# Unit 0's window mask as a bias added by matmuls, zero matmuls that wait for results, and a new order of work

## The chip, the cores and the metric

The kernel runs on one core of one Trainium2 chip. The metric is the device time of one execution in microseconds (us). Before the change three runs gave 165.78, 166.09 and 166.78 us, so the median is 166.09 us.

The engines are named as the profile names them: PE (TensorE matmul), PEld (its weight load), DVE (VectorE), ACT (ScalarE), POOL (GpSimd) and SP (SyncE, which here only starts transfers).

## The reference

Attention with 4 sink keys and a window of 128 keys, for 4 batches, 8 heads, 768 positions and heads of 64, and then a channel mix on the attention's output:

```python
scores = q @ k.T / 8
keep = (key < 4) | ((0 <= query - key) & (query - key < 128))
a = softmax(where(keep, scores, -1e9));  x = a @ v          # x: [4, 768, 512]
x_prev = x shifted by one position, zeros first
xk = mu_k * x + (1 - mu_k) * x_prev;  xr = mu_r * x + (1 - mu_r) * x_prev
k = relu(xk @ w_k);  v = (k * k) @ w_v;  out = sigmoid(xr @ w_r) * v
```

`w_k` is 512 x 1024, `w_v` is 1024 x 512, `w_r` is 512 x 512. All inputs and the output are float32; the kernel multiplies in bfloat16.

## The kernel before

**Units.** The work is cut into 12 units of 256 positions, three for each batch (T = 0, 1, 2). For each unit u the kernel does four steps.

- `prepare(u)`: k and q arrive in float32 (tiles ks, qs), are cast to bfloat16 (kb, qb), and are transposed into kt and qt. For early units PE transposes and an engine copies the result out of PSUM (lines 726 and 721); from unit 5 (k) and 7 (q) on a DMA transposes. v is cast to vb (line 740).
- `attend(u)`: for each of four pairs of heads, scores into a PSUM tile `sc` (line 815), exp on ACT (line 887, tile e), a product with a 0/1 mask on DVE (line 901), probabilities times values on PE (line 920), a reciprocal and a scaling on DVE (lines 934 and 937, tile x). A unit with T = 0 has a mask of 384 columns for each of two heads (`mask0`), the others one of 256 columns repeated. Sink keys go their own small way (lines 784, 791, 858 or 873).
- `mix(u)`: x is transposed (line 961, copied out at line 970 into xt), then differences td (line 997) and the fused multiply-adds xk and xr (line 1010), all on DVE.
- `ffn(u)`: keys (line 1087), relu (line 1097 on ACT or 1101 on DVE), square (line 1109, DVE), gate (line 1118), tanh (line 1124, ACT), product with w_v (line 1136), and the gating (line 1145, DVE), then the store (line 1152). The second half of the last unit is cut in two column parts (`last_product`, lines 1046 to 1074): 128 columns first, then 384.

The weights come as float32 and are cast by pieces: four of w_k and two of w_r (lines 620 and 626), four of w_v (lines 620 and 624).

**Order.** Nothing is issued where the code defines it. Every step is registered with `P.op` under a running number. `CHOICE` (line 18) gives an engine to the numbers that may run on several, and `ORDER` (line 72) has, for each of PE, DVE, ACT, POOL and SP, the complete sequence of numbers by hand. `Plan.schedule` (line 187) merges these five sequences with estimated costs, hands out the buffers on the way, and each engine then runs its own sequence strictly in order, waiting for semaphores where a step needs another engine's result.

**Zero matmuls.** Where the plan sees PE idle for more than 300 ns (600 ns early on) before 26 us of its own clock, it puts in matmuls of a zero tile `warm` (lines 1160 to 1166) into a free PSUM bank. They wait for no result; they only keep PE running.

**Constants.** POOL builds the identity, the masks, and small tiles for the sinks at the start, in the order mask0, identity, hmask, mask, spread, and casts the second half of unit 0's k after them. DVE clears tiles in `fill` and `fill_later` (lines 525 to 537, some 2 us).

The code of `BIAS` (line 38, the function `biased`, the functions `make_bias0` and `first_mask`) is there before the change, but the tuple is empty, so no unit uses it.

Of the kernel before, what the change touches and what calls it, by code (L numbers as in the profile page):

```python
# [18 lines left out]
    80: "ACT", 81: "POOL", 82: "ACT", 83: "POOL", 84: "POOL", 85: "ACT", 86: "ACT",  # L19
    88: "ACT", 90: "DVE", 96: "POOL", 98: "DVE", 99: "DVE", 101: "DVE", 102: "ACT",  # L20
    103: "ACT", 129: "POOL", 132: "DVE", 135: "POOL", 141: "ACT", 144: "DVE", 151:
    "DVE", 160: "PE/full", 172: "PE/full", 183: "POOL", 186: "DVE", 189: "POOL",
    192: "POOL", 195: "ACT", 196: "DVE", 198: "DVE", 242: "PE/full", 265: "DVE",
    268: "DVE", 271: "POOL", 273: "DVE", 274: "POOL", 277: "DVE", 278: "ACT", 352:
    "POOL", 355: "POOL", 361: "DVE", 380: "DVE", 428: "POOL", 432: "POOL", 438:
    "ACT", 496: "PE/full", 511: "POOL", 516: "ACT", 517: "ACT", 587: "POOL", 591:
    "ACT", 592: "ACT", 628: "POOL", 661: "POOL", 663: "POOL", 665: "ACT", 666:
    "ACT", 675: "DVE", 736: "POOL", 741: "ACT", 785: "POOL", 810: "POOL", 815:
    "DVE", 855: "POOL", 888: "DVE", 889: "ACT", 929: "POOL", 945: "PE/full", 998:
    "DVE", 1002: "DVE", 1006: "DVE", 1010: "DVE", 1019: "POOL",  # L30
# [7 lines left out]
BIAS = ()  # L38
# [56 lines left out]
    ),  # L95
    "DVE": (
# [25 lines left out]
    ),  # L122
    "ACT": (
# [14 lines left out]
    ),  # L138
    "POOL": (
# [3 lines left out]
    ),  # L143
# [8 lines left out]
    ),  # L152
}


class Plan:

    SEM = 40.0
    LAG = {"PE": 163.0, "DVE": 83.0, "ACT": 114.0, "POOL": 60.0, "SP": 90.0}

    def __init__(self):
        self.ops, self.pools, self.buf = [], {}, {}
        self.fill, self.fill_until = None, 0.0  # L170

# [15 lines left out]
    def schedule(self):  # L187
# [43 lines left out]
        while any(lines.values()):  # L231
# [35 lines left out]
            if o["port"]:  # L267
                port[o["engine"]] = t + (0.58 * cost if o["engine"] == "POOL" else cost)
# [953 lines left out]
```

## Time and profile before

| what | value |
|---|---|
| median of three runs | 166.09 us |
| the profiled execution | 166.53 us |
| its span, first to last instruction | 164.4 us |
| PE busy | 152.6 us, 93% of the span |
| DVE busy | 149.5 us, 91% |
| ACT busy | 121.7 us, 74% |
| POOL busy | 31.7 us, 19% |
| matmuls, weight loads | 1819, 1838 |

The profiled execution has 2.13 us around its span and is 0.44 us above the median. Numbers of the trace are compared within that one execution.

The page gives the busy time of each engine, the span in 40 slices with the busy tenths of each engine and the clock that was granted to PE, the DMA queues, the chain of waits that ended last, and the costliest groups of instructions. A matmul's recorded time is a latency: 512 columns take 379 ns from start to end, but eight of them follow one another in 1.73 us. So a PE that looks busy still has some room.

### The profile page before, as it was taken

The numbers are of one execution on the slowest core, as the hardware profiler recorded it, in microseconds if no ns is written. First come the engines' busy times: TensorE is split into PE (matmuls) and PEld (weight loads), VectorE is DVE, ScalarE is ACT, GpSimd is POOL, SyncE is SP. The second block draws the span as 40 slices with busy tenths as digits, with TensorE's granted clock in tenths as the row PEclk, the third lists the DMA queues.
The fourth block names the chain that finished last, engine by engine and source line by source line (L and its number), as shares of the span: only waits on it lengthen the run. The fifth ranks groups of instructions, "written<-read, shape, count | busy, mean of one in ns | idle before, by whom it ended". The sixth has DMA issues, their size and how long they took to land.

```text
span 164.4 us, 4647 instructions
## 1 busy us (share of the span) xinstructions
PE 152.6 (93%) x1819; PEld 101.1 (61%) x1838; DVE 149.5 (91%) x383; ACT 121.7 (74%) x198; POOL 31.7 (19%) x61
## 2 busy tenths in 40 slices
PE   7988678899989999999999999999999999999991
PEld 2445557675448658677666766855485756578450
DVE  2599999999999999999999999998899989999931
ACT  3789989999989999999997689782499695152020
POOL 6633341312422023220201001032000100101001
PEclk9999789999999999999999999999999999999999
DMA  5999998999899999889988998999999933251032
GB/s 145 249 357 278 394 333 215 366 394 322 193 271 272 260 219 221 160 176 162 270 216 207 233 232 215 220 219 128 235 165 191 268 94 96 54 205 64 0 144 112
DMA packets 78821, 35.16 MB, mean 214 GB/s; under 512 B 68744, under 2 KB 71056, under 8 KB 78800
## 3 DMA queue, kind: packets, MB, share of 16 engines
q1 hardware_dynamic: 78384, 33.56, 84.0%
q0 software_dynamic: 400, 1.31, 2.3%
q8 instruction: 14, 0.23, 0.6%
q14 instruction: 7, 0.06, 0.1%
q10 hardware_dynamic: 16, 0.00, 0.0%
HBM read 24.12 MB, written 6.29 MB: 185 GB/s over the span
## 4 chain that ended last, share of the span: by engine, by line
PE 62%; DVE 24%; DMA 4%; POOL 4%; issue 3%; ACT 1%; DVEq 0%; POOLq 0%
PE bank L1087 21%; PE bank L1136 18%; PE bank L1118 8%; PE bank L920 6%; DVE e L901 5%; DMA kt<-kb 4%; PE sc L815 4%; DVE xr L1010 3%; DVE xk L1010 3%; DVE x L937 3%; DVE kk L1109 2%; DVE td L997 2%; PE bank L873 1%; POOL hmask L543 1%; PE bank L1057 1%
## 5 line engine op out<-in xcount | busy, mean ns | idle before, releaser
L1087 PE MATMUL bank<-xk,wk_sb 128*128 128x256 bf16 x384 | 47.6, 273 | 1.1 <-ACT rl L1097 0.5
L887 ACT ACTIVATE e<-sc 128x1024 bf16<-128x1024 f32 (+1 forms) x48 | 44.5, 967 | 2.8 <-PE sc L815 2.5
L1136 PE MATMUL bank<-wv_h,kk 128*128 128x512 bf16 x171 | 43.8, 379 | 0.8 <-DVE xk L1010 0.2
L1087 PEld LDWEIGHTS <-wk_sb 128*128 128x128 bf16 x384 | 36.2, 98 | 7.7 <-issue 1.5
L1097 ACT ACTIVATE rl<-bank 128x512 bf16<-128x512 f32 x43 | 25.2, 607 | 8.3 <-PE bank L1087 7.8
L901 DVE TENSOR_TENSOR e<-e,mask 128x1024 bf16<-128x1024 bf16 (+1 forms) x48 | 30.8, 656 | 0.0
L1124 ACT ACTIVATE th<-bank 128x512 f32<-128x512 f32 x24 | 14.3, 612 | 18.2 <-PE bank L1118 11.4
L1136 PEld LDWEIGHTS <-kk 128*128 128x128 bf16 x184 | 17.0, 98 | 16.5 <-issue 0.2
L1010 DVE SCALAR_TENSOR_TENSOR xr<-td,mu_all,xt 128x256 bf16<-128x256 bf16 x48 | 23.8, 507 | 0.0
L1118 PE MATMUL bank<-wr_sb,xr 128*128 128x512 bf16 x90 | 23.3, 379 | 0.3
L1010 DVE SCALAR_TENSOR_TENSOR xk<-td,mu_all,xt 128x256 bf16<-128x256 bf16 x48 | 23.3, 511 | 0.0
L1109 DVE TENSOR_TENSOR kk<-rl 128x512 bf16<-128x512 bf16 x48 | 19.8, 425 | 0.4 <-ACT rl L1097 0.2
L937 DVE TENSOR_TENSOR x<-bank,rec 128x256 bf16<-128x256 f32 x48 | 19.5, 418 | 0.4
L920 PE MATMUL bank<-vb,e 128*128 128x65 bf16 x352 | 16.8, 196 | 1.4 <-DVE e L901 1.1
L1145 DVE SCALAR_TENSOR_TENSOR ob<-th,bank 128x512 f32<-128x512 f32 x23 | 15.6, 681 | 1.9 <-PE bank L1136 1.1
L920 PEld LDWEIGHTS <-e 128*128 128x128 bf16 x352 | 14.2, 99 | 4.5 <-DVE e L901 1.9
L1118 PEld LDWEIGHTS <-xr 128*128 128x128 bf16 x96 | 9.0, 98 | 9.6
L815 PE MATMUL sc<-qt,kt 64*64 64x128 bf16 (+3 forms) x496 | 12.5, 226 | 0.1
L1152 POOL DMA_DIRECT2D out_dram<-ob x5 | 2.8, 570 | 46.8 <-DVE ob L1145 46.8
L815 PEld LDWEIGHTS <-kt 64*64 64x64 bf16 (+1 forms) x496 | 9.0, 106 | 3.3 <-issue 1.0
L997 DVE TENSOR_TENSOR td<-xt 128x512 bf16<-128x512 bf16 x24 | 10.1, 432 | 0.1
L663 POOL CAST kb<-ks 128x512 bf16<-128x512 f32 x6 | 5.3, 884 | 20.4 <-DMA ks<-in_k_dram 17.8
(87 smaller groups left out, 157.2 us busy)
## 6 DMA issues: line engine op xcount, KB each, us to landing
vs<-in_v_dram SPq DMA_DIRECT2D x24, 256.0 KB, 5.3
out_dram<-ob SPq DMA_DIRECT2D x18, 256.0 KB, 3.3
ks<-in_k_dram SPq DMA_DIRECT2D x16, 256.0 KB, 4.2
qs<-in_q_dram SPq DMA_DIRECT2D x12, 256.0 KB, 4.9
qs<-in_q_dram SPq DMA_DIRECT2D x6, 512.0 KB, 7.1
ks<-in_k_dram SPq DMA_DIRECT2D x4, 512.0 KB, 9.3
w<-in_moe_w_k_dram SPq DMA_DIRECT2D x2, 1024.0 KB, 8.6
w<-in_moe_w_v_dram SPq DMA_DIRECT2D x2, 1024.0 KB, 10.6
```

The costliest lines, as they stand in the source:

```text
L815: nc.tensor.matmul(out=sc[keys, a, o0 + f0 - q0:o0 + f1 - q0], lhsT=lhs[rows, keys], rhs=qs[rows, f0:f1], start=u not in BIAS, stop=True, ...
L887: nc.scalar.activation(out=buf[ek][:, :, lo:], in_=buf[sck][:, :, lo:], func=AF.Exp, scale=scale)
L901: nc.vector.tensor_tensor(out=at, in0=at, in1=m, op=ALU.mult)
L920: nc.tensor.matmul(out=o[:, g, a, :], lhsT=e[:, a, e0:e0 + 128], rhs=rhs, start=(T == 0 and i == 0), stop=(i == len(blocks) - 1), skip_gro ...
L937: P.op("DVE", dve(256), lambda ok=ok, rk=rk, c=c: nc.vector.tensor_tensor(out=buf["x", u][:, :, 128 * c:128 * c + 128].rearrange("p g (a d ...
L1010: nc.vector.scalar_tensor_tensor(out=buf[key][:, c, :], in0=buf[tk][:, i, :], scalar=mu[w][:, c:c + 1], in1=xt[:, c, t0 - 1:t0 + 255], op0 ...
L1087: nc.tensor.matmul(out=ps[:, i, :], lhsT=wk_sb[:, c, 128 * f:128 * f + 128], rhs=xk[:, c, :], start=(c == 0), stop=(c == NC - 1), skip_gro ...
L1097: nc.scalar.activation(out=buf[rk], in_=buf[psk].rearrange("p (i t) -> p i t", i=2), func=AF.Relu)
L1109: P.op("DVE", dve(512, 0.52), lambda f2=f2, rk=rk: nc.vector.tensor_tensor(out=buf["kk", u][:, 2 * f2:2 * f2 + 2, :], in0=buf[rk], in1=buf ...
L1118: nc.tensor.matmul(out=buf[psk], lhsT=buf["xr", u][:, c, 128 * g:128 * g + 128], rhs=wr_sb[:, c, :], start=(c == 0), stop=(c == NC - 1))
L1136: nc.tensor.matmul(out=buf[psk], rhs=wv_h[:, f, :], lhsT=buf["kk", u][:, f, 128 * g:128 * g + 128], start=(f == 0), stop=(f == NF - 1))
L1145: P.op("DVE", dve(512), lambda psk=psk, tk=tk, bk=bk: nc.vector.scalar_tensor_tensor(out=buf[bk], in0=buf[tk], scalar=1.0, in1=buf[psk], o ...
```

## The change

- `BIAS = (0,)`: for unit 0 POOL builds a tile `bias0` of 384 columns (0 where a key is seen, -30000 where not) in a buffer of `ob` that is used much later. For each pair of score tiles PE first multiplies the identity with that tile into `sc`, two matmuls for each score tile, eight in all, and the score matmuls add to it. The four mask products of unit 0 on DVE are gone. `mask0` is still made, for units 3, 6 and 9, after unit 0's cast on POOL, and so are `mask` and `spread`.
- Zero matmuls from 4.6 us of the plan's clock on can have a `gate`: the moving operand is then not the zero tile but a tile that a step on DVE or ACT has just written, so that the matmul waits for that step. The stationary operand stays zero. They may go into a free bank or a free score tile. The plan leaves 130 ns behind each (`PAUSE`), and goes on with them to 28.5 us of its clock.
- Costs of the plan: POOL casts 600 instead of 620 ns, weight casts on POOL 1050 instead of 1100, a store from POOL 600 instead of 1100, DMA transposes 2250 (k) and 1450 (q) instead of 1950.
- `CHOICE` and all five sequences of `ORDER` are new. SP's first 15 transfers keep their order; from there on the loads of w_r and w_v stand behind more loads of k, q and v.

The numbers after 72 are shifted by one, those after unit 0's attention by minus one. With that taken out, these steps change their engine (counts over the whole kernel, before and after):

| step (line) | ACT | DVE | POOL |
|---|---|---|---|
| mask product (901) | | 48, 44 | |
| cast of unit 0's k, q (668) | 1, 3 | 2, 0 | 1, 1 |
| cast of k, q, units 1 to 4 and q of 5, 6 (659) | 7, 8 | 4, 2 | 9, 10 |
| cast of k, q of DMA-transposed units (663) | 16, 15 | 0, 1 | 8, 8 |
| copy of kt, qt (721) | 19, 18 | 1, 2 | |
| cast of v (740) | 14, 13 | 4, 2 | 6, 9 |
| cast of w_k, w_r (626) | 3, 2 | | 3, 4 |
| cast of w_v (624) | 2, 3 | 2, 1 | |
| copy of xt (970) | 9, 10 | 5, 4 | |
| relu (1096) | 43, 42 | 5, 6 | |

The first-half copies of unit 0's kt and qt (line 726) go from ACT to DVE and the second-half ones from DVE to ACT. Seven stores instead of five start from POOL. In the last unit the 384-column part now stands ahead of the 128-column part.

```diff
-BIAS = ()
+BIAS = (0,)
...
+    PAUSE = 130.0
...
+        done = {}
...
+                own.append((b[0], name, b[1], None))
...
-            if o["engine"] == "PE" and self.fill:
+            if o["engine"] == "PE" and self.fill and before < 4600.0:
...
+            elif o["engine"] == "PE" and self.fill and before < self.fill_until:
+                last = max((j for j in o["after"]), key=lambda j: ops[j]["end"], default=None)
+                now, seen = before, before - 500.0
+                while now + 230.0 < t:
+                    some = [(b[0], name, b[1], b) for name in ("bank", "sc") for b in free[name]
+                            if b[0] <= now] + [b for b in own if b[1] in ("bank", "sc") and b[0] <= now]
...
+                    gates = [j for j, e in done.items() if seen < e + self.SEM <= now and (
+                        last is not None and ops[j]["engine"] == ops[last]["engine"] or
+                        e < t - 700.0)]
+                    gate = max(gates, key=lambda j: done[j], default=None)
...
+                    order.append(("fill", tile_ if name == "bank" else tile_[:, 0, :], 1, gate))
+                    now += 225.0
...
+                    now += self.PAUSE if gate is not None else 0.0
+            if o["engine"] in ("DVE", "ACT") and self.gate(i):
+                done[i] = end
...
+    def part(i):
...
+        if name == "wk":
+            return lambda: wk_sb[:, 0, 256 * u:256 * u + 128]
...
+        if name == "xt":
+            t0 = 16 + 256 * key[2]
+            return lambda: xts[u][:, 2 * key[3], t0:t0 + 128]
...
+    def fill(bank, wide, gate=None):
+        if gate is not None:
+            nc.tensor.matmul(out=bank, lhsT=warm[:, 0:128], start=True, stop=True,
+                             rhs=part(gate)().unsqueeze(1).to_broadcast([128, 4, 128]))
...
-    P.fill_until = 26000.0
+    P.fill_until = 28500.0
```

More of the change, by code (lines that the diff above doesn't have):

```diff
@@ L18 @@
 CHOICE = {
[L19 to L30, printed above, removed]
+    81: "ACT", 82: "POOL", 83: "POOL", 84: "POOL", 85: "ACT", 86: "POOL", 87: "ACT",
+    89: "ACT", 90: "ACT", 93: "DVE", 96: "DVE", 97: "POOL", 104: "ACT", 128: "DVE",
+    134: "POOL", 137: "POOL", 141: "ACT", 171: "PE/full", 182: "POOL", 185: "POOL",
+    187: "DVE", 194: "ACT", 195: "DVE", 197: "DVE", 204: "DVE", 216: "DVE", 253:
+    "PE/full", 264: "POOL", 267: "POOL", 270: "DVE", 275: "DVE", 276: "ACT", 282:
+    "DVE", 289: "DVE", 345: "POOL", 348: "POOL", 354: "POOL", 358: "ACT", 396:
+    "POOL", 404: "PE/full", 427: "POOL", 428: "POOL", 431: "DVE", 436: "ACT", 437:
+    "ACT", 510: "POOL", 515: "ACT", 584: "POOL", 585: "POOL", 590: "ACT", 627:
+    "POOL", 631: "POOL", 703: "POOL", 734: "POOL", 735: "POOL", 740: "ACT", 741:
+    "ACT", 771: "DVE", 780: "POOL", 813: "ACT", 814: "DVE", 841: "DVE", 858:
+    "PE/full", 881: "POOL", 885: "POOL", 888: "ACT", 924: "POOL", 944: "PE/full",
+    977: "DVE", 994: "POOL", 1001: "DVE", 1005: "DVE",
 }
@@ L254, in schedule @@
             lines[o["engine"]].pop(0)
+            own = []
             for name, key in o["take"]:
@@ L267, in schedule @@
             if o["port"]:
-                port[o["engine"]] = t + (0.58 * cost if o["engine"] == "POOL" else cost)
+                port[o["engine"]] = t + (max(0.58 * cost, cost - 200.0) if o["engine"] == "POOL" else cost)
             end = t + cost + o["lag"]
@@ L311, in schedule @@
                     order.append(("fill", self.pools["bank"][b[1]], wide))
+            elif o["engine"] == "PE" and self.fill and before < self.fill_until:
[4 more added lines that the diff above has]
+                            if b[0] <= now] + [b for b in own if b[1] in ("bank", "sc") and b[0] <= now]
+                    if not some:
+                        now += 60.0
+                        continue
+                    _, name, at_, b = min(some, key=lambda b: b[:3])
+                    tile_ = self.pools[name][at_]
+                    gates = [j for j, e in done.items() if seen < e + self.SEM <= now and (
[3 more added lines that the diff above has]
+                    if gate is not None:
+                        seen = done[gate] + self.SEM
+                    order.append(("fill", tile_ if name == "bank" else tile_[:, 0, :], 1, gate))
+                    now += 225.0
+                    if b is not None:
+                        free[name].remove(b)
+                        free[name].append((now, at_))
+                    now += self.PAUSE if gate is not None else 0.0
+            if o["engine"] in ("DVE", "ACT") and self.gate(i):
+                done[i] = end
             order.append(i)
@@ L630, in cast @@
                    "ACT": (act(1024), emit("ACT"), False)} |
-             ({} if half else {"POOL": (1100.0, emit("POOL"), True)}),
+             ({} if half else {"POOL": (1050.0, emit("POOL"), True)}),
              reads=[(name + "32", i)], writes=writes)
@@ L676, in prepare @@
                            "DVE": (341.0, cast(nc.vector.tensor_copy), True),
-                           "POOL": (620.0, cast(nc.gpsimd.tensor_copy), True)},
+                           "POOL": (600.0, cast(nc.gpsimd.tensor_copy), True)},
                      take=[] if half else [(name + "b", rk)],
@@ L1155, in ffn @@
                  alts={"SP": (400.0, store(nc.sync), False),
-                       "POOL": (1100.0, store(nc.gpsimd), True)})
+                       "POOL": (600.0, store(nc.gpsimd), False)})
     zeros = warm.bitcast(FP32)
-    def fill(bank, wide):
-        if wide == 1:
+    def part(i):
+        o = P.ops[i]
+        key = o["writes"][0] if o["writes"] else ()
+        if not isinstance(key, tuple) or len(key) < 2:
+            return None
+        name, u = key[0], key[1]
+        if name == "wk":
+            return lambda: wk_sb[:, 0, 256 * u:256 * u + 128]
+        if name == "wr":
+            return lambda: wr_sb[:, 2 * u, 0:128]
+        if name == "wv":
+            return lambda: wv_h[:, 2 * u, 0:128]
+        if name == "e" and o["engine"] == "DVE":
+            return lambda: buf[key][:, 0, 384:512]
+        if name in ("kb", "qb") and not by_dma(name[0], u):
+            if octet(name[0], u):
+                return lambda: eights(buf[key[:2]])[:, 4 * key[2]].rearrange("p h d -> p (h d)")
+            return lambda: buf[key[:2]][:, 0, 4 * key[2]:4 * key[2] + 2, :].rearrange(
+                "p h d -> p (h d)")
+        if name == "x":
+            return lambda: buf["x", u][:, 0, 128 * key[2]:128 * key[2] + 128]
+        if name == "xt":
+            t0 = 16 + 256 * key[2]
+            return lambda: xts[u][:, 2 * key[3], t0:t0 + 128]
+        if name == "td":
+            return lambda: buf[key][:, 0, 0:128]
+        if name in ("xk", "xr") and len(key) == 3:
+            return lambda: buf[key[:2]][:, key[2], 0:128]
+        if name == "rl":
+            return lambda: buf[key][:, 0, 0:128]
+        if name == "kk":
+            return lambda: buf["kk", u][:, 2 * key[2], 0:128]
+        return None
+    def fill(bank, wide, gate=None):
+        if gate is not None:
+            nc.tensor.matmul(out=bank, lhsT=warm[:, 0:128], start=True, stop=True,
+                             rhs=part(gate)().unsqueeze(1).to_broadcast([128, 4, 128]))
+        elif wide == 1:
             nc.tensor.matmul(out=bank, lhsT=warm[:, 0:128], start=True, stop=True,
```

11 lines of the change are left out of this document (6 added, 5 removed), and 140 rows, old and new, of the table ORDER.

## The prediction

> **What bounds the kernel now.** I read the page's head and its 40 slices first, then the busy time of each engine by stage, because shares over the whole span mix stages.
>
> ```profile
> span 164.4 us, 4647 instructions
> PE 152.6 (93%) x1819; PEld 101.1 (61%) x1838; DVE 149.5 (91%) x383; ACT 121.7 (74%) x198; POOL 31.7 (19%) x61
> PEclk9999789999999999999999999999999999999999
> ...
> 0.00:9.55 9.55, 8.04 (x37) 3.64 (x37) 4.76 (x21) 5.72 (x9) 5.83 (x24) 1.00 0.83 209
> 9.55:45.36 35.81, 30.59 (x425) 21.52 (x427) 35.40 (x85) 32.93 (x53) 11.98 (x17) 0.95 1.04 318
> 45.36:100.00 54.64, 53.53 (x734) 37.24 (x742) 53.99 (x141) 49.48 (x84) 8.60 (x11) 1.00 1.02 221
> 100.00:157.00 57.00, 56.54 (x606) 36.77 (x612) 53.85 (x138) 32.76 (x55) 4.77 (x9) 1.00 0.70 155
> ```
>
> The columns of the stages are length, then busy PE, PEld, DVE, ACT, POOL, granted clock, DMA share, GB/s. I cut where the chain of waits changes hands: from DVE's first mask product (9.55 us) to its first `ob` (45.36) nearly all its links are DVE. There DVE is busy 35.40 of 35.81 us and ACT 32.93, so ACT has 2.9 us to spare; PE idles 5.2 us. From 45.36 to 100 PE idles 1.1 and DVE 0.65 us: both are full. After 100 only PE is. So a microsecond saved on DVE counts up to 45 us, is shared with PE to 100, and hardly counts later; POOL is nearly free throughout.
>
> What feeds the start is data:
>
> ```profile
> 3.87 0.51 DVE L668 CAST kb<-ks 128x512 bf16<-128x512 f32 x1 [2.04 <-DMA ks<-in_k_dram]
> 4.59 1.04 DVE L531 MEMSET vsink<- 128x520 bf16 x2
> 6.27 0.43 DVE L668 CAST qb<-qs 128x512 bf16<-128x512 f32 x1
> 7.24 0.61 POOL L668 CAST kb<-ks 128x512 bf16<-128x512 f32 x1 [1.29 <-DMA ks<-in_k_dram]
> 8.34 0.69 DVE L726 COPY kt<-bank 128x512 bf16<-128x512 bf16 x1 [1.64 <-PE bank L708]
> 8.95 0.68 DVE L726 COPY qt<-bank 128x512 bf16<-128x512 bf16 x1
> 9.55 0.55 DVE L901 TENSOR_TENSOR e<-e,mask 128x768 bf16<-128x768 bf16 x1
> 10.82 1.16 POOL L659 CAST kb<-ks 128x512 bf16<-128x512 f32 x2 [1.21 <-DMA ks<-in_k_dram]
> 21.06 1.04 POOL L626 CAST wk_sb<-w 128x1024 bf16<-128x1024 f32 x1 [2.23 <-DMA w<-in_moe_w_k_dram]
> 24.34 0.38 PE L1087 MATMUL bank<-xk,wk_sb 128*128 128x256 bf16 x2
> ```
>
> The casts wait for k's halves at 3.87 and 7.24 us, for unit 1's k at 10.82 and for w_k at 21.06, and the first FFN matmul stands at 24.34. SP's first 15 transfers are unchanged, so these dates stay.
>
> **DVE's sum.** The moved steps have one price each by form:
>
> ```profile
> L901 DVE TENSOR_TENSOR e<-e,mask 128x768 bf16<-128x768 bf16 x16 | 8.9, 572 | 0.0
> L740 DVE CAST vb<-vs 128x512 bf16<-128x512 f32 x4 | 1.7, 420 | 0.0
> L970 DVE COPY xt<-bank 128x512 bf16<-128x512 bf16 x5 | 2.0, 410 | 0.0
> L721 DVE COPY kt<-bank 128x512 bf16<-128x512 bf16 x1 | 0.7, 677 | 0.0
> L624 DVE TENSOR_SCALAR wv_h<-w 128x1024 bf16<-128x1024 f32 x2 | 1.4, 682 | 0.0
> L1101 DVE TENSOR_SCALAR rl<-bank 128x512 bf16<-128x512 f32 x5 | 3.3, 686 | 0.3 <-PE bank L1087 0.3
> L740 ACT CAST vb<-vs 128x512 bf16<-128x512 f32 x14 | 8.7, 635 | 0.5 <-DMA vs<-in_v_dram 0.4
> ```
>
> (I give the L740 price, 0.42, to the equal casts of L659 and L663.) Following both sequences up to the first `ob`, DVE loses four masks (2.29), unit 0's two casts (0.51 + 0.43), five casts of q of units 1 to 3, k of 3 and v of 3 (2.10), three copies of xt (1.23), one of kt (0.68), a piece of w_v (0.68) and a relu (0.69): 8.61 us. It gains two casts of k (0.84; units 1 and 3), two copies of qt (1.36), three of xt (1.23), a relu (0.69) and one cast of unit 5 (0.42): 4.54. The copies of unit 0's kt and qt are exchanged one for one. Net -4.1 us.
>
> Of this, what DVE did before 10.8 us saves nothing. In the new sequence it waits from `fill` for kt's transposes (about 5 us), copies kt and qt, only then clears its tiles (2 us, over by 8.5), and the next step is the cast of unit 1's k, which lands at 10.8. In that time the old order had done the two casts and two masks of unit 0 (0.94 + 1.1); so 2.0 of the 4.1 us are lost in a wait, and **-2.1 us** is left.
>
> **POOL's price on DVE.** The new order puts casts on POOL. What that does is seen here:
>
> ```profile
> L1010 DVE SCALAR_TENSOR_TENSOR xr<-td,mu_all,xt x48: 456/477/1250, 16.5 to 152.9; 128x256 bf16<-128x256 bf16 x48
> ...
> 21.13 1.25 DVE L1010 SCALAR_TENSOR_TENSOR xr<-td,mu_all,xt 128x256 bf16<-128x256 bf16 x1
> ...
> 17.20 1.63 POOL L659 CAST kb<-ks 128x512 bf16<-128x512 f32 x2 [0.89 <-DMA ks<-in_k_dram]
> ...
> 17.23 1.12 DVE L901 TENSOR_TENSOR e<-e,mask 128x1024 bf16<-128x1024 bf16 x1
> 18.28 0.41 DVE L970 COPY xt<-bank 128x512 bf16<-128x512 bf16 x1
> ```
>
> Beside the cast of w_k (1.04 us from 21.06) a DVE step with a median of 0.477 takes 1.25, so 0.77 is lost; the mask beside a small cast takes 1.12 against 0.68 elsewhere, 0.44 lost; the copy out of PSUM at 18.28 keeps its 0.41 beside the same POOL work. Up to 45 us POOL has 16 casts in place of 14, one of the two extra ones a weight: 0.77 + 0.44 = **+1.2 us**. `mask0` and `mask` also move to after 11 us (1.7 us of POOL work by the rows at L543 and L562 below); DVE's steps there read PSUM (L934, L937), which lose nothing, so I take 0, with +1.0 as the other end.
>
> [...] Taken at full length for each POOL microsecond, the two casts and the moved masks would be 1.6 + 1.7 = 3.3 us and not 1.2; that case is the third rival.
>
> **ACT.** Up to 45 us ACT gets 16 small steps and gives up 13, at 0.6 us (the L740 row) +1.8, and two weight pieces change against two others. Its spare 2.9 us falls to about 1.0. So even if DVE gained more, ACT lets little over 1 us through. Most of what it takes on belongs to units 0 to 2, ahead of 24 us, where its rows (below, at 16 to 24) already show 3.83 and 3.29 busy of 4.
>
> **PE.** The eight bias matmuls:
>
> ```profile
> 1.29 0.80 POOL L543 TENSOR_SCALAR_AFFINE_SELECT mask<-ones 128x128 bf16<-128x128 bf16 x3 [0.77 <-DVE ones L527]
> 2.05 0.30 POOL L562 MEMSET mask<- 4x256 bf16 x1
> 9.35 0.38 PE L1162 MATMUL bank<-warm 128*128 128x512 bf16 x1
> 159.41 1.46 PE L1057 MATMUL bank<-wv_h,kk 128*128 128x384 bf16 x8
> 160.91 0.55 DVE L1067 SCALAR_TENSOR_TENSOR ob<-th,bank 128x384 f32<-128x384 f32 x1 [0.55 <-PE bank L1057]
> ```
>
> Eight of 384 columns take 1.46 us (the row at 159.41, same width), half ahead of each pair of scores, in time that zero matmuls fill today (9.35). They need only the identity and `bias0` (0.80 + 0.30 on POOL, in `mask0`'s old place): 0, and 0.7 if the second four stand behind a late POOL. PE's first step is now the small transpose of mu; its two 2 KB loads are issued at 1.1 and 1.7 us, and everything PE does waits behind it: 0, up to +0.5.
>
> Zero matmuls with a wait: behind each stands all of PE's queue, so the next real step can lose the 0.38 us of L1162 or, if the awaited result is late, the lateness. PE's idle 5.2 us in the stage from 9.55, at 0.36 us a piece (225 + 130 ns in the plan), hold about 14 of them. Between nothing (all in real gaps) and 14 x 0.38 = +5.3 (all on the path) I take 0, nearest to DVE's row: it is full to 45 us and hides what PE does late by less than its queue. They could also gain:
>
> ```profile
> 16.00:20.00 4.00, 2.39 (x52) 2.12 (x52) 4.00 (x8) 3.83 (x7) 1.94 (x3) 0.83 1.05 396
> 20.00:24.00 4.00, 2.93 (x55) 2.18 (x53) 3.85 (x11) 3.29 (x6) 1.27 (x2) 0.74 1.10 360
> ```
>
> Clock 0.83 and 0.74 lose (0.17 + 0.26) x 4 = 1.7 us of PE's time, but DVE is idle 0.15 us in those 8, so at most 0.15 comes back: 0. [...] If PE were the path there, the sum would be 1.7 us lower.
>
> **Later steps.** Loads of w_r and w_v stand behind 2 to 6 more loads on SP. The first product with w_v moves from PE's place 70 to 92, so the later data has cover; without it a PE wait of some us. Stores move between SP and POOL late, where both are idle: 0. After 45 us DVE's net change is nil and ACT's -1.9: 0, with 1.5 either way for an order that differs everywhere. At the end 128 columns stand last in place of 384: the last DVE step shrinks from 0.55 us to about 0.29 (same step, other part): **-0.2**.
>
> **The sum.** -2.1 + 1.2 - 0.2 = -1.1 us, and the -0.9 of it that lies on DVE is just what ACT's spare 1.0 lets through. The profiled execution (166.53) becomes 165.4; it lies 0.44 above the median, so I forecast **165.0**, with a range of its own from 164.2 to 165.9.
>
> **Rivals.**
> - *More goes through (faster).* DVE's 2.0 us before 10.8 return because unit 0's x is ready without masks, and the steadier clock gives PE its 1.7 us at 16 to 24. For it: DVE's total falls 4 us and both engines are full to 100 us. Against: ACT. -4.1 + 1.2 - 0.2 = -3.1 is 163.0 against the median; with 0.7 of the clock's share it is 162.3, with only half of the 2.0 returned 164.0. So 162.3 to 164.2. Chance 0.30.
> - *The waiting zero matmuls hold PE (slower).* Where real results run later than the plan by more than a gap, all 14 block scores and values, ACT's exps start later, and ACT has no slack to catch up. Half of them at 0.38 is 2.7 us, all 5.3; less the 1.1: 167.7 to 170.3. It decides (slower by over 1%) once more than 7 of them cost their full length. For it: ACT full to 24 us, strict order. Against: DVE's queue. Chance 0.24.
> - *POOL holds DVE, nothing is gained.* With 3.3 for 1.2 the sum is +1.0: 166.0 to 167.2. The 0.41 us copy at 18.28 speaks against it. Chance 0.10.
>
> **The numbers.** Forecast 0.36, of which 0.05 lies under 164.4. About 1% (1.7 us) is what a measurement here tells from no change. Faster: 0.30 + 0.05; slower: 0.23 of the second rival's 0.24; the rest is the same. The range leaves out a tenth at each end: 162.4 to 168.2.
>
> **What would show it.** In the new profile: four fewer mask steps; DVE idle about 2 us before 10.8; stage 16 to 24 at clock 1.00; the first FFN matmul still at 24 to 25; DVE steps at L1010 over 1 us beside weight casts; PE idle under 1.1 us in the 55 us after the first `ob`. I am wrong if PE waits on ACT or DVE in rows of the zero matmuls, if ACT's waits for scores grow, or if PE's idle time after 45 us moves by over 1.5 us.

## The result, and the profile after

The changed kernel takes **171.86 us** (median of six runs), the kernel before 165.94 us on the same chip: ratio 1.0319, 95% interval 1.0272 to 1.0366. It is slower by 3.2%, about 5.3 us. The ratio is taken without the executions in which the chip was in a slower state, 1 to 2% longer here, so it is not the quotient of the two medians. The forecast was 165.0 us with a range up to 168.2, so both the sign and the range were wrong. The profiled execution has a span of 170.2 us against 164.4. In the new file the lines are those of before plus 30 (the mask product is line 931, the exp 917, the scores 845); the biased products are line 854, the zero matmuls with a wait line 1226, those without 1229 and 1232.

The head of the page and its clock row:

```profile
span 170.2 us, 4708 instructions
PE 156.0 (92%) x1845; PEld 102.2 (60%) x1865; DVE 149.3 (88%) x374; ACT 121.3 (71%) x198; POOL 38.4 (23%) x72
...
PEclk9999999999999999999999999999999999999999
```

The clock is now full throughout, and DVE's busy time over the whole kernel is what it was (149.5). The same stages as before, with the same columns (length, busy PE, PEld, DVE, ACT, POOL, granted clock, DMA share, GB/s):

```profile
0.00:9.55 9.55, 6.12 (x29) 3.12 (x29) 4.08 (x19) 3.40 (x6) 5.00 (x19) 1.00 0.80 192
9.55:45.36 35.81, 31.08 (x454) 21.50 (x453) 31.50 (x73) 32.88 (x54) 16.66 (x30) 1.00 1.09 327
45.36:100.00 54.64, 52.91 (x708) 35.06 (x717) 52.55 (x132) 49.53 (x82) 9.54 (x14) 1.00 0.93 200
100.00:157.00 57.00, 56.06 (x601) 37.03 (x608) 54.61 (x139) 33.83 (x56) 6.16 (x10) 1.00 0.79 164
```

Between 9.55 and 45.36 us DVE is busy 31.50 us where it was busy 35.40. The four microseconds that were to be saved are there, but as idle time, and the kernel is late. The first stage shows why to look at the start: ACT is busy 3.40 us instead of 5.72, among others because the first exps have all but left it. The timeline of that start (start, duration, engine, line, operation; in brackets the idle time before it and what ended it):

```profile
5.77 0.69 DVE L756 COPY kt<-bank 128x512 bf16<-128x512 bf16 x1 [3.93 <-PE bank L738]
6.45 0.69 DVE L756 COPY qt<-bank 128x512 bf16<-128x512 bf16 x1
...
7.35 1.04 DVE L561 MEMSET vsink<- 128x520 bf16 x2
...
8.75 0.31 DVE L567 MEMSET sc<- 64x128 f32 x2
...
9.11 0.51 PE L845 MATMUL sc<-qt,kt 64*128 64x256 bf16 x8 [1.83 <-DVE sc L567]
...
9.48 1.51 ACT L917 ACTIVATE e<-sc 128x768 bf16<-128x768 f32 x2 [2.09 <-PE sc L845]
...
11.29 0.43 DVE L689 CAST kb<-ks 128x512 bf16<-128x512 f32 x1 [2.17 <-DMA ks<-in_k_dram]
```

kt and qt of the first scores are there at 7.14 us. But the scores are written to a tile of which DVE clears a corner, and this clear (0.31 us, line 567) stands last in `fill_later`, which the new order places behind the two copies. So the first scores start at 9.11 us. By the code, unit 0's scores and exps use only the columns from 128 on, and the clear those from 64 to 127: the scores wait for the tile, not for values that they need. Before, the same rows were:

```profile
6.00 0.31 DVE L537 MEMSET sc<- 64x128 f32 x2
6.48 0.51 PE L815 MATMUL sc<-qt,kt 64*128 64x256 bf16 x8
6.86 1.51 ACT L887 ACTIVATE e<-sc 128x768 bf16<-128x768 f32 x2 [0.43 <-PE sc L815]
```

The first exp is 2.6 us late. In the list of PE's waits (columns: engine, line waited for, total, times, longest) this one stands first, and those of the waiting zero matmuls are small:

```profile
PE sc L845 <- DVE sc L567: 1.8, 1, 1.8
PE bank L950 <- DVE vb L770: 1.7, 2, 1.2
...
PE bank L1226 <- DVE xr L1040: 0.6, 1, 0.6
```

The 2.6 us don't explain 5.3 by themselves. Following DVE's written order through the traces gives the dates at which its last scaling of a unit (the `x` step) ends:

| kernel | unit 0 | unit 1 | unit 2 | unit 5 | unit 9 | last `ob` of all |
|---|---|---|---|---|---|---|
| before | 17.3 | 26.9 | 38.8 | 74.9 | 116.5 | 161.5 |
| after | 15.9 | 27.5 | 42.4 | 81.5 | 123.5 | 167.2 |
| a_sc_early (below) | 13.8 | 24.6 | 37.8 | 76.7 | 119.7 | 162.1 |
| b_fill_early (below) | 17.5 | 26.2 | 38.4 | 74.8 | 116.1 | 162.0 |
| b_sc_late (below) | 22.1 | 30.7 | 42.9 | 79.2 | 120.4 | 165.3 |
| b_pool21 (below) | 17.4 | 26.2 | 38.2 | 78.2 | 121.2 | 166.8 |
| b_bias (below) | 17.1 | 26.9 | 39.7 | 75.7 | 117.2 | 162.1 |

(Old and new order take the units in different turns, so rows of one order are to be compared with each other.)

### The profile page after: what moved, and what is told of

The parts are those of the page before. It is cut to its first block, busy times and chain, and to the rows that moved or that the text cites. A ratio compares the mean times of both kernels' runs of the same rounds, so it can differ in the third digit from the quotient of the medians.

```text
span 170.2 us, 4708 instructions
## 1 busy us (share of the span) xinstructions
PE 156.0 (92%) x1845; PEld 102.2 (60%) x1865; DVE 149.3 (88%) x374; ACT 121.3 (71%) x198; POOL 38.4 (23%) x72
## 4 chain that ended last, share of the span: by engine, by line
PE 61%; DVE 25%; ACT 6%; issue 3%; DMA 2%; DVEq 0%; ACTq 0%
PE bank L1166 21%; PE bank L1117 17%; PE bank L1148 9%; DVE e L931 7%; PE bank L950 5%; PE sc L845 4%; DVE xk L1040 3%; DVE xr L1040 3%; DVE x L967 3%; ACT e L917 3%; DVE kk L1139 2%; DMA ob<-in_moe_mu_k_dram 2%; PE bank L991 1%; DVE td L1027 1%; DVE rec L964 1%
## 5 line engine op out<-in xcount | busy, mean ns | idle before, releaser
L917 ACT ACTIVATE e<-sc 128x1024 bf16<-128x1024 f32 (+1 forms) x48 | 45.0, 963 | 6.7 <-PE sc L845 5.0
L1117 PE MATMUL bank<-xk,wk_sb 128*128 128x256 bf16 x384 | 48.8, 273 | 0.6 <-DVE xk L1040 0.3
L931 DVE TENSOR_TENSOR e<-e,mask 128x1024 bf16<-128x1024 bf16 (+1 forms) x44 | 31.3, 715 | 0.8 <-ACT e L917 0.8
L1127 ACT ACTIVATE rl<-bank 128x512 bf16<-128x512 f32 x42 | 24.3, 606 | 9.9 <-PE bank L1117 9.0
L1040 DVE SCALAR_TENSOR_TENSOR xk<-td,mu_all,xt 128x256 bf16<-128x256 bf16 x48 | 24.8, 534 | 0.1
L1040 DVE SCALAR_TENSOR_TENSOR xr<-td,mu_all,xt 128x256 bf16<-128x256 bf16 x48 | 24.4, 518 | 0.0
L950 PE MATMUL bank<-vb,e 128*128 128x65 bf16 x352 | 17.2, 193 | 2.4 <-DVE vb L770 1.7
L950 PEld LDWEIGHTS <-e 128*128 128x128 bf16 x352 | 14.5, 97 | 6.0 <-issue 2.2
L845 PE MATMUL sc<-qt,kt 64*64 64x128 bf16 (+4 forms) x496 | 12.6, 226 | 2.3 <-DVE sc L567 1.8
L1182 POOL DMA_DIRECT2D out_dram<-ob x7 | 3.9, 564 | 44.1 <-DVE ob L1175 38.0
L770 POOL CAST vb<-vs 128x512 bf16<-128x512 f32 x9 | 6.5, 728 | 24.2 <-DMA vs<-in_v_dram 24.1
L964 DVE RECIPROCAL rec<-bank 128x4 f32<-128x4 f32 x48 | 7.9, 172 | 3.3 <-PE bank L950 2.6
```

The costliest lines, as they stand in the source:

```text
L845: nc.tensor.matmul(out=sc[keys, a, o0 + f0 - q0:o0 + f1 - q0], lhsT=lhs[rows, keys], rhs=qs[rows, f0:f1], start=u not in BIAS, stop=True, ...
L917: nc.scalar.activation(out=buf[ek][:, :, lo:], in_=buf[sck][:, :, lo:], func=AF.Exp, scale=scale)
L931: nc.vector.tensor_tensor(out=at, in0=at, in1=m, op=ALU.mult)
L950: nc.tensor.matmul(out=o[:, g, a, :], lhsT=e[:, a, e0:e0 + 128], rhs=rhs, start=(T == 0 and i == 0), stop=(i == len(blocks) - 1), skip_gro ...
L1040: nc.vector.scalar_tensor_tensor(out=buf[key][:, c, :], in0=buf[tk][:, i, :], scalar=mu[w][:, c:c + 1], in1=xt[:, c, t0 - 1:t0 + 255], op0 ...
L1117: nc.tensor.matmul(out=ps[:, i, :], lhsT=wk_sb[:, c, 128 * f:128 * f + 128], rhs=xk[:, c, :], start=(c == 0), stop=(c == NC - 1), skip_gro ...
```

## The experiments

Names that begin with a_ are made from the changed kernel, those with b_ from the kernel before. Where an old order is used with the new code, its numbers are mapped to the new numbering.

### Is it the place of the clear, or is it the zero matmuls, the bias, the order?

a_sc_early is the changed kernel with nothing altered but the place of the two clears:

```diff
     def fill():
         for t, value in ((ones, 1.0), (spread, 0.0), (hmask, 1.0)):
             nc.vector.memset(t, value)
+        for t in P.pools["sc"]:
+            nc.vector.memset(t[0:64, :, 64:128], 0.0)
 
     def fill_later():
...
-        for t in P.pools["sc"]:
-            nc.vector.memset(t[0:64, :, 64:128], 0.0)
```

> The changed kernel, with the two clears of the score tiles (0.31 us on DVE) moved from the end of fill_later to the end of fill, ahead of the copies of kt and qt. Late start theory: the first scores no longer wait for DVE (1.8 us in the changed kernel), the first exp starts at about 7.2 us and not 9.5, and the whole is 1.0 to 2.5 us shorter. If POOL's casts or the zero matmuls are the cause, the first exp comes early but the whole changes by under 0.7 us.

Measured: 167.38 us, ratio 1.0075 (1.0038 to 1.0112). Moving a clear of 0.31 us takes back 2.4 of the 3.2%. Its timeline:

```profile
1.86 0.31 DVE L559 MEMSET sc<- 64x128 f32 x2
...
6.95 0.51 PE L845 MATMUL sc<-qt,kt 64*128 64x256 bf16 x8
...
7.32 1.51 ACT L917 ACTIVATE e<-sc 128x768 bf16<-128x768 f32 x2 [0.49 <-PE sc L845]
```

The scores come 2.2 us earlier than in the changed kernel, unit 0's `x` 2.1, unit 1's 2.9, unit 2's 4.6 us; from there to the end the distance stays between 3.8 and 5.1. So the lateness of the start more than doubles between 25 and 42 us.

a_no_zero leaves the changed kernel as it is, without a zero matmul after 4.6 us:

```diff
-    P.fill_until = 28500.0
+    P.fill_until = 0.0
```

> The changed kernel without any zero matmul after 4.6 us of the plan's clock. If the zero matmuls that wait hold PE, the whole is 2 to 5 us shorter. If they lie in real gaps, it is the same within 0.7 us or, since PE's clock can then fall in the first 30 us, up to 1.5 us longer.

Measured: 171.70 us, ratio 1.0315 (1.0229 to 1.0401), the same as with them. The clock of PE falls (to 0.51 from 20 to 24 us), and in the whole this costs nothing that these runs can tell. Unit 1's `x` ends at 28.2 us instead of 27.5, as DVE waits longer for PE (the row `DVE rec L964 <- PE bank L950` has 3.7 us between 11 and 43 us, against 2.0 in the changed kernel), but unit 2's ends at 42.4 in both:

```profile
20.00:24.00 4.00, 2.91 (x43) 2.47 (x43) 3.45 (x8) 3.80 (x6) 1.11 (x1) 0.51 1.05 390
```

b_bias is the kernel before with the bias alone, b_zero the changed code in the old order without the bias (so that only the zero matmuls with their waits and pauses are new), b_bias_zero the changed code with both in the old order.

```diff
-BIAS = ()
+BIAS = (0,)
```

> The kernel before, with unit 0's masks as bias matmuls and its old order otherwise: the bias matmuls directly ahead of each pair of scores, the four mask products gone from DVE's sequence, bias0 in mask0's place on POOL and mask0 behind unit 0's small sink copies. By my sum this saves what DVE loses after 9.5 us: up to 2.2 us of masks, and 1 to 2 us of the whole if DVE bounds to 45 us; nothing (within 0.7 us) if the arrival of data or ACT sets the pace. If the bias itself is what costs, it is 1 us or more longer.

> The changed code with the old sequences, the old choice of engines and no bias: the zero matmuls that wait are the one thing that is new beside the plan's costs. If they hold PE, 1 to 4 us longer than before; if they lie in gaps, the same within 0.7 us, with PE's clock at 1.00 from 16 to 24 us.

> The changed code with bias and waiting zero matmuls, but the old sequences and engines (mapped to the new numbers, the masks of unit 0 left out). If the halved PE clock at 21 to 29 us is what took the gain from the bias alone, the clock is 1.00 and the whole 0.7 to 1.5 us shorter than before. If unit 0's masks were hidden anyway, the same within 0.7 us. If bias and zero matmuls together hold PE, 1 us or more longer.

Measured: b_bias 0.9987 (0.9941 to 1.0033), b_zero 1.0004 (0.9966 to 1.0042), b_bias_zero 0.9986 (0.9942 to 1.0030). The waiting zero matmuls neither hold PE nor bring anything, although they keep its clock up; the row of b_zero over 16 to 24 us:

```profile
16.00:24.00 8.00, 5.96 (x114) 3.93 (x110) 8.00 (x17) 7.44 (x12) 3.31 (x5) 1.00 1.02 378
```

Its first scores stand 0.9 us later than before (6.48 us), without loss:

```profile
7.34 0.50 PE L843 MATMUL sc<-qt,kt 64*128 64x256 bf16 x8
```

Nor do the four masks less bring anything by themselves. The stage from 9.55 to 25 us in b_bias, and who DVE waits for in it:

```profile
9.55:25.00 15.45, 10.40 (x198) 7.83 (x197) 13.11 (x33) 13.29 (x22) 7.62 (x13) 0.88 1.10 341
```

```profile
DVE rec L931 <- PE bank L917: 1.0, 1, 1.0
DVE xt L967 <- PE bank L958: 0.7, 1, 0.7
DVE qb L656 <- DMA qs<-in_q_dram: 0.6, 1, 0.6
```

The same stage of the kernel before, where DVE waits for nothing that is listed:

```profile
9.55:25.00 15.45, 11.34 (x201) 8.22 (x201) 15.12 (x36) 13.55 (x22) 6.54 (x9) 0.89 1.11 343
```

DVE does 2.0 us less work and is idle for just that much longer, and unit 2's `x` ends at 39.7 instead of 38.8 us. So in the old order the bias, the zero matmuls and the two together cost nothing; what makes the changed kernel slow is in its order, with its choice of engines. (The bias was not taken out of the new order by itself.)

### Is a late first score enough to make the old order slow?

If the date of the first scores is the cause, delaying it in the old order must cost as much. b_fill_early is the control: the other clears go into `fill`, where DVE waits for data anyway, and the clear of the score tiles stays behind the cast of k.

```diff
     def fill():
...
+        for t in ksink + vsink:
+            nc.vector.memset(t, 0.0)
+        for t in P.pools["vb"]:
+            nc.vector.memset(t[:, :, :, D:D + 1], 1.0)
+        for t in xts:
+            nc.vector.memset(t[:, :, 0:16], 0.0)
 
     def fill_later():
-        for t in ksink + vsink:
-            nc.vector.memset(t, 0.0)
-        for t in P.pools["vb"]:
-            nc.vector.memset(t[:, :, :, D:D + 1], 1.0)
-        for t in xts:
-            nc.vector.memset(t[:, :, 0:16], 0.0)
         for t in P.pools["sc"]:
             nc.vector.memset(t[0:64, :, 64:128], 0.0)
```

b_sc_late puts six clears of a spare tile ahead of that clear, and `fill_later` (71) one place later on DVE. In both the plan also lets unit 0's scores come behind `fill_later`.

```diff
     def fill_later():
+        for _ in range(6):
+            nc.vector.memset(spare, 0.0)
         for t in P.pools["sc"]:
             nc.vector.memset(t[0:64, :, 64:128], 0.0)
...
-        70, 90, 71, 99, 98, 101, ...
+        70, 90, 99, 71, 98, 101, ...
```

> The kernel before, with the clears of the sink tiles, of vb's ones and of xt's edges moved out of fill_later into fill, so that DVE does them in the 2.0 us in which it waits for the first k, and the clear of the score tiles alone stays behind the cast of k. It is the control of the next kernel. Theory (the first scores' date is what counts, and here qt's copy on ACT sets it, not the clear): the first scores stay at 6.4 to 6.6 us, q's second cast comes up to 1.5 us earlier, and the time is within 0.5% of before, ratio 0.992 to 1.005. Rival (any change of DVE's early order costs, since the later order was fitted to it): over 1.01.

> As the control, but the clear of the score tiles stands behind q's second cast and behind six clears of a spare tile (0.5 us each), which nothing reads. Nothing else of the old order is touched; the first scores should stand at 8.7 to 9.3 us instead of 6.5. Theory (the date of the first scores and exps alone makes most of the loss): the delay of 2.3 to 2.8 us passes through to the end, ratio 1.013 to 1.024 against the kernel before. Rival (the delay costs only together with the new order, which puts POOL casts beside two-input steps of DVE; the old order takes up the lateness in its waits for data): below 1.007.

Measured: b_fill_early 166.53 us, ratio 1.0019 (0.9984 to 1.0054); b_sc_late 170.58 us, ratio 1.0286 (1.0245 to 1.0327). The control's start and the delayed one's:

```profile
4.40 0.30 DVE L537 MEMSET sc<- 64x128 f32 x2
...
6.67 0.50 PE L815 MATMUL sc<-qt,kt 64*128 64x256 bf16 x8
```

```profile
6.39 0.43 DVE L669 CAST qb<-qs 128x512 bf16<-128x512 f32 x1 [2.01 <-DMA qs<-in_q_dram]
...
10.71 0.30 DVE L538 MEMSET sc<- 64x128 f32 x2
...
11.32 0.81 ACT L888 ACTIVATE e<-sc 128x768 bf16<-128x768 f32 x1 [4.02 <-PE sc L816]
```

The delay came out longer than planned, 4.3 us (exp at 11.32 instead of 7.05 us in the control), because q's second cast waits for its data until 6.39 us and each spare clear waits 0.17 us for the one before. By the two ratios the kernels lie 2.7% apart, about 4.4 us. In the table they stay 4.3 to 4.6 us apart from unit 0 to unit 9; in these two executions about 1 us of it is made good after that. So in the old order a late first score goes through to the end at about its full length. A smaller one need not, as b_zero's 0.9 us show.

The spare clears also keep DVE itself busy until 11.01 us, past the time at which the control copies the second half of kt. In b_sc_late that copy, once DVE is free, still waits for PE, whose queue the first scores have held up; the control's row and the delayed one:

```profile
8.57 0.69 DVE L726 COPY kt<-bank 128x512 bf16<-128x512 bf16 x1 [1.74 <-ACT e L887]
...
12.03 0.69 DVE L727 COPY kt<-bank 128x512 bf16<-128x512 bf16 x1 [1.01 <-PE bank L709]
```

So the scores set the date of this copy, but without them DVE's own clears would still have made it up to 2.4 of these 3.5 us later. Of the two tests a_sc_early is the clean one.

### Where do the other two microseconds come from?

Between 25 and 42 us the late kernel meets POOL at another place. POOL's casts wait for data (the cast of w_r's piece starts at 33.63 us here and at 33.44 in a_sc_early), but DVE is by then 3 us behind. POOL in the changed kernel:

```profile
33.63 1.04 POOL L656 CAST wr_sb<-w 128x1024 bf16<-128x1024 f32 x1 [4.54 <-DMA w<-in_moe_w_r_dram]
34.61 1.82 POOL L689 CAST qb<-qs 128x512 bf16<-128x512 f32 x2
36.38 0.80 POOL L689 CAST kb<-ks 128x512 bf16<-128x512 f32 x1
```

and DVE beside it:

```profile
33.73 1.21 DVE L1040 SCALAR_TENSOR_TENSOR xr<-td,mu_all,xt 128x256 bf16<-128x256 bf16 x1
34.87 1.09 DVE L931 TENSOR_TENSOR e<-e,mask 128x1024 bf16<-128x1024 bf16 x1
35.88 0.83 DVE L770 CAST vb<-vs 128x512 bf16<-128x512 f32 x1
36.63 1.09 DVE L931 TENSOR_TENSOR e<-e,mask 128x1024 bf16<-128x1024 bf16 x1
...
38.32 0.48 DVE L1040 SCALAR_TENSOR_TENSOR xr<-td,mu_all,xt 128x256 bf16<-128x256 bf16 x1
```

In a_sc_early POOL does the same casts in nearly the same microseconds, but DVE is elsewhere in its order:

```profile
31.86 0.68 DVE L931 TENSOR_TENSOR e<-e,mask 128x1024 bf16<-128x1024 bf16 x1
...
33.70 0.42 DVE L967 TENSOR_TENSOR x<-bank,rec 128x256 bf16<-128x256 f32 x1
...
34.24 0.42 DVE L967 TENSOR_TENSOR x<-bank,rec 128x256 bf16<-128x256 f32 x1
```

Four steps of the changed kernel are 0.73, 0.41, 0.41 and 0.41 us longer than the same forms beside no cast (0.48, 0.68, 0.42, 0.68): 2.0 us in one run of casts. In a_sc_early the steps there that read PSUM keep their 0.42. Summed over all DVE steps that lie beside POOL work (length less the median of the same form without such company), up to 45 us DVE loses 4.6 us in the changed kernel, 1.9 in a_sc_early and 5.0 before. The 2.7 us between the first two fit the growth of the lateness from 2.1 to 4.6 us. As DVE's sequence is the same in both, the lag can also be followed step by step: it is 3.2 us ahead of the four longer steps and 5.2 behind them, and then falls to 4.3, as a_sc_early meets casts of its own. a_no_zero has the same four steps (1.19, 1.09, 0.83 and 1.09 us) and the same lag. The sums alone would prove little: b_fill_early loses 3.3 us up to 45 us where before loses 5.0, and takes the same time. So this part of the account is read from traces; no run here moves those casts away from the late DVE.

That such losses can reach the end was tested by itself. b_pool21 is the kernel before with 21 casts of a spare tile on POOL, three behind each of seven of its casts between 46 and 87 us, in POOL's idle time; nothing reads them.

```diff
+                if i in (428, 432, 511, 518, 587, 663, 736):
+                    self.idle_casts()
...
+    def idle_casts():
+        for _ in range(3):
+            nc.gpsimd.tensor_copy(out=spare16, in_=spare32)
```

> The kernel before with 21 more casts of 512 columns on POOL, three each behind seven of its steps from 44 to 90 us, from a tile that nothing else uses: 12.9 us of POOL work in POOL's idle time. By the old trace's average (5.7 us lost on DVE beside 29.4 us of POOL work) DVE loses 2.5 us and the whole 1 to 2.5 us; if POOL's work takes DVE's time one for one, DVE loses 8 to 12 us and the whole 5 us or more; if it costs nothing, the same within 0.5 us.

Measured: 171.64 us, ratio 1.0313 (1.0225 to 1.0400): casts that take 12.9 us by themselves, put into POOL's idle time, cost 5.3 us of the kernel, where at most 2.5 were expected from the average of the old trace. POOL and DVE at one such place:

```profile
65.44 2.58 POOL L1175 CAST spare<-spare 128x512 bf16<-128x512 f32 x3
...
71.49 0.61 POOL L665 CAST kb<-ks 128x512 bf16<-128x512 f32 x1
```

```profile
65.44 0.76 DVE L939 TENSOR_TENSOR x<-bank,rec 128x256 bf16<-128x256 f32 x2
66.11 0.68 DVE L903 TENSOR_TENSOR e<-e,mask 128x1024 bf16<-128x1024 bf16 x1
66.71 0.83 DVE L1012 SCALAR_TENSOR_TENSOR xr<-td,mu_all,xt 128x256 bf16<-128x256 bf16 x1
67.47 1.09 DVE L903 TENSOR_TENSOR e<-e,mask 128x1024 bf16<-128x1024 bf16 x1
...
70.99 0.68 DVE L1147 SCALAR_TENSOR_TENSOR ob<-th,bank 128x512 f32<-128x512 f32 x1
```

Steps that read SBUF alone go from 0.47 to 0.83 us and from 0.68 to 1.09; the steps with an input from PSUM keep their time (means over the whole kernel: `x` 0.417 us, before 0.418; `ob` 0.680, before 0.681). Not every meeting lengthens the DVE step: the mask product at 66.11 keeps its 0.68 us, and the cast that starts with it takes 1.16. Summed as above, DVE loses 11.2 us instead of 5.7, and the kernel is longer by about that difference. POOL's casts are stretched too, to 0.86 us from 0.61 in these rows; over the whole kernel POOL's busy time goes from 31.7 to 48.0 us. So in these rows both sides get longer; what makes them do so the traces don't show. DVE's loss of 5.5 us is less than half of the 12.9 us that the casts take by themselves, as some DVE steps beside them keep their time.

### A gap in the transfers

In the changed kernel the DMA transpose of unit 5's k heads SP's queue before its cast has been made, and the loads behind it stand still; in slice 13 of the page the DMA engines move 4 GB/s. The wait on SP's queue:

```profile
SPq L715 <- DVE kb L693: 7.4, 1, 7.4
```

a_kt5 moves that transpose back on SP in the changed kernel, behind the load numbered 30 (three places; the expectations say five), a_sc_kt5 does the same to a_sc_early.

> The changed kernel with that transpose five places later in SP's sequence and nothing else (the clear stays late). If the gap in the transfers at 51 to 55 us carries the loss, 1.5 to 4 us shorter than the changed kernel. If the late first scores carry it, under 1 us.

> The changed kernel with the early clear of the score tiles, and the DMA transpose of unit 5's k five places later in SP's sequence, behind loads that it held up (SP stood from 46.7 to 50.6 us waiting for DVE's cast of that k). If that wait is what is left of the loss, 0.7 to 1.3 us shorter than with the early clear alone and about equal to the kernel before. If what is left lies in the new order elsewhere, the same within 0.6 us.

Measured: a_kt5 170.84 us, 1.0255 (1.0166 to 1.0343); a_sc_kt5 168.30 us, 1.0116 (1.0037 to 1.0194). The gap is filled in a_kt5 (206 GB/s from 51 to 55 us), and the gain is within the intervals; beside the early clear it is nil. So the gap is not a cause worth a per cent that can be told.

### What is left, and where the saving goes

a_sc_early is still 0.75% above before, where b_bias_zero, with the same bias and zero matmuls in the old order, is level. a_sc_t45 and a_sc_t80 are a_sc_early with all steps that the plan of before starts after 45 or 80 us put back into the old order and on the old engines.

> The changed kernel with the early clear, in which all steps that the plan of before starts after 45 us stand in the old order, on the old engines; the steps ahead of them stay in the new order. Theory (the remaining 0.75% is lost by the new order of the later steps, since useful work of PE was 0.7 us ahead of before at 45 us and 1 us behind from 120 on): ratio 0.993 to 1.000. Rival (it is a debt of the start, such as buffers and loads that come late): 1.005 to 1.010 as before.

> The same with the cut at 80 us of the plan of before. Theory that the residue is lost after 80 us: ratio 0.995 to 1.002. If it is lost between 45 and 80 us: 1.004 to 1.010, while the cut at 45 us recovers it. If neither cut recovers it, it is a debt of the start.

Measured: a_sc_t45 170.69 us, 1.0260 (1.0211 to 1.0310); a_sc_t80 167.69 us, 1.0101 (1.0058 to 1.0145). Neither recovers it. The cut at 80 us changes nothing that can be told, so the new order of the last half isn't what costs; the cut at 45 us costs 1.9% beside a_sc_early, as if the two halves didn't fit, so it says nothing of the stretch between. Which part of the new order holds the 1.2 us stays open.

In its profiled execution b_bias_zero stood 1.4 us ahead of before from 45 to 77 us and gave it back by 107. To see whether transfers take such a lead back, the stores of units 0 to 5 were cut to 32 of 512 columns in both, b_light and bz_light (less to transfer; the rest of these units' output is left out), or six stores of 77 to 96 us were started from POOL, b_pool_st and bz_pool_st (a shorter queue on SP):

```diff
-                return lambda: queue.dma_start(out=out[b, s0:s0 + 128, :], in_=buf[bk])
+                w = 32 if u < 6 else Dm
+                return lambda: queue.dma_start(out=out[b, s0:s0 + 128, 0:w], in_=buf[bk][:, 0:w])
```

```diff
 CHOICE = {
+    323: "POOL", 397: "POOL", 401: "POOL", 476: "POOL", 480: "POOL", 558: "POOL",
```

> The kernel before, whose stores of units 0 to 5 carry only 32 of 512 columns (16 KB instead of 256 KB, 12 stores between 47 and 111 us); the rest of these units' output is left out. It is the control of bz_light. Theory that transfers set the pace only once DVE has been relieved: ratio 0.993 to 1.000. If transfers already hold the kernel before: below 0.990.

> b_bias_zero (the changed code with bias and waiting zero matmuls in the old order), with the same 12 stores cut to 32 columns. With full stores its steps stood 1.4 us ahead of before from 45 to 77 us and level with it from 107 us on. Theory (transfers take the lead back: from 76 us on ACT's casts wait for v and k, 0.8 us each, in a stretch where the DMA engines are busy throughout): with less to transfer the lead of 1.0 to 1.4 us stays to the end, a ratio lower than that of b_light by 0.006 to 0.009. Rival (PE and DVE are full from 80 us on and take it back whatever arrives when): the ratio of b_light, within 0.003.

> The kernel before with six stores of 77 to 96 us started from POOL instead of SP, in POOL's idle time; nothing left out. It is the control of bz_pool_st. Expected within 0.3% of before: SP has waits of about 2 us in that stretch.

> b_bias_zero with the same six stores moved from SP to POOL; as many bytes as before. SP's queue is busy there without a gap. If the place in SP's queue delays the loads of v and k (4 us of stores stand ahead of them), part of the lead of 1.4 us stays: ratio 0.991 to 0.995, the first version under both kernels. If the DMA engines themselves are the limit: 0.997 to 1.001.

Measured: b_light 1.0012 (0.9989 to 1.0035), bz_light 1.0051 (1.0014 to 1.0089), b_pool_st 1.0021 (0.9995 to 1.0047), bz_pool_st 1.0057 (1.0014 to 1.0101). The theory falls: with less to transfer the bias gains nothing either. And the lead it was to explain isn't there in general: unit 2's `x` ends at 39.7, 37.5, 39.0 and 39.1 us in the four profiled kernels with the bias in the old order (b_bias, b_bias_zero, bz_light, bz_pool_st), at 38.8, 38.4, 38.9, 38.2 and 37.7 in five without it (before, b_fill_early, b_zero, b_pool21, b_light). The lead was one execution's start, which varies by 1 to 2 us among these. No kernel here beats the one before.

## Why the prediction was wrong, point by point

- **The step that failed** is the one on DVE's start: "copies kt and qt, only then clears its tiles (2 us, over by 8.5)", priced as 2.0 us of DVE's time lost in a wait. The sequence was right to 0.6 us (the clears end at 9.06), the wait before unit 1's cast was 2.17 us as forecast. But the step was only asked what it costs DVE, not who waits for what it writes. The last of its clears releases the first scores. Their lateness of 2.6 us was priced at nothing. Moving the clear ahead is worth 2.4%, with nothing else changed, and delaying it by six spare clears in the old order costs 2.7%.
- **DVE's net -4.1 us**: the size was right, its worth was not. There are 44 masks instead of 48, and DVE's busy time in the stage from 9.55 fell by 3.9 us. Half of it was to come through. In b_bias the saved 2.0 us are waits for PE and for data, and the time is the same; DVE's 35.40 of 35.81 us were read as the bound; that it was full didn't mean that less work would let it go on sooner.
- **ACT's spare time**: in the changed kernel it stays at 2.9 us (32.88 busy), as ACT starts late. Without that lateness the step held. a_sc_early's two parts of the stage have ACT busy 15.29 of 15.45 and 19.88 of 20.36 us, a spare of 0.6 where 1.0 was forecast:

```profile
9.55:25.00 15.45, 14.52 (x231) 9.16 (x229) 13.16 (x36) 15.29 (x25) 8.05 (x17) 1.00 1.07 351
25.00:45.36 20.36, 19.59 (x276) 14.25 (x276) 20.03 (x50) 19.88 (x35) 8.03 (x12) 1.00 1.10 305
```

- **POOL's price**, +1.2 us up to 45 us: the price of a collision was right (0.73 and 0.41 us lost in the rows at 33.73 and 34.87, 0.77 and 0.44 forecast), but counting casts doesn't say how many collide. Up to 45 us DVE lost 4.6 us in place of 5.0, with more casts; the same casts cost 1.9 us in a_sc_early. The third rival (nothing gained, 166.0 to 167.2) named this engine, but not that a late DVE would move into the casts. That DVE loses one microsecond for each of POOL's, from which its 3.3 us come, no run shows: in b_pool21 12.9 us of casts cost DVE 5.5.
- **Bias matmuls at 0, mu's transpose first, waiting zero matmuls at 0, clock at 0**: right. b_bias and b_zero are level with before; mu's transpose waited 0.46 us for its load, at the end of the range given; it ended at 4.77 us, and the first cast of k at 4.55, so it held PE by some 0.2 us. The second rival, zero matmuls that hold PE, had the right sign for the wrong reason: the longest wait in their rows is 0.6 us, and without them the time is the same. That the higher clock could bring 1.7 us is not borne out here: full clock brought nothing in b_zero, and about half the clock from 20 to 24 us cost the whole nothing in a_no_zero.
- **Later steps**, 0 with 1.5 us either way: a_sc_early holds 1.2 us (0.75%) that no run here places. The 7.4 us wait of SP's queue was not foreseen; what a_kt5 gained, 0.6%, lies within the intervals.
- **The tail**, -0.2 us: from PE's last product (164.87 + 1.91 us) to the end of the span are 3.4 us, before 3.5. The sign was right, the size 0.1.
- **Of what was to show it**: the first FFN product, which was to stay at 24 to 25 us, stands at 26.32, and ACT's waits for scores, whose growth was named as a sign against the forecast, are 5.0 us in place of 2.5 over the whole span.

```profile
ACT e L917 <- PE sc L845: 5.0, 5, 2.1
```

## What to carry to other kernels

When a step is moved, price it twice: what it takes from its own engine, and for each tile that it writes, who waits for that tile; a memset of 0.3 us at the end of a bundle of clears can hold the first product of the whole kernel. In an order written out by hand a late start can be paid more than once, as in the changed kernel: the engines keep their sequences, data and casts keep their dates, and steps that were fitted around each other collide. An engine that is busy for 99% of a stage may be fed at that rate, so take some of its work away alone before counting the saving.

## What was not expected of the hardware

POOL's idle time was not free: 21 casts of 0.61 us that nothing reads, in its gaps, lengthened the kernel by 5.3 us. In the rows shown, most DVE steps that read SBUF alone were 0.36 to 0.41 us longer beside such a cast (0.83 for 0.47, 1.09 for 0.68), and steps that read PSUM were not (`ob` 0.68 with and without it). PE at about half its clock (0.51 from 20 to 24 us) cost nothing that can be measured in the whole time (1.0315 against 1.0319).
